# Linear-attention chunks with a MoE behind them: operands spread by matmuls in place of DRAM round trips, and more columns streamed ahead of the steps

## Chip, cores and metric

One core of a Trainium2 chip runs the whole program in one launch. The metric is device microseconds (us) of that core; the fewer the better.

## The reference

Three stages follow one another. The first is a recurrence over 768 time steps for 4 x 8 heads of width 40; the second a MoE layer with one of eight experts per token; the third a gated product with dense weights. Only the first stage is touched here.

```python
state = zeros(B, H, D, D)                     # 4, 8, 40, 40
for t in range(768):
    y[t]  = r[t] @ state
    Sa    = state @ a[t]
    state = state * w[t] - outer(Sa, b[t]) + outer(v[t], k[t])
x   = y reordered to (3072, 320)
x   = gate(x) * (relu(x @ w1[e(x)]) @ w2[e(x)])   # e(x): the expert of a token
out = ((x @ w_a) * (x @ w_b)) @ w_out
```

## The kernel before, in words

The recurrence is cut into 12 chunks of 64 time steps. Within a chunk the steps become matrix products: a Gram matrix of the decayed operands, the inverse of a triangular matrix made of it, and products with the state that the chunk before left. Each chunk `c` goes through these functions of the class `Attn`:

- `load` (L129) fetches the five operands `w a k b r` into tiles `raw0` to `raw4`, one buffer each. `cum` (L141) makes running products of `w` on VectorE (the scans of L151).
- `prod` (L164) multiplies `a`, `k`, `b` by these products (L174), splits each into two float16 halves (ScalarE: L177, L184, L191; GpSimd: L120, L185) and writes the halves from the tiles `ara`, `kb` and `arr` to DRAM (L171). Further DRAM writes are `dg` (L197) and `dds` (L205).
- `fetch` (L233) and `rfetch` (L214) read the halves back through `spread` (L211), three DMAs per tensor. The read puts them in another layout: a head's 40 rows stand three times, in the high-low pairing that the float16 products want, in the tiles `a3`, `kb3` and `r3`. `fetch` also reads `dds` into `DT` (L245), and `gtr` (L219) reads `dg` into `dl` (L222).
- `gram` (L248) makes the Gram matrix `gm` on TensorE (L256), masks it on VectorE (L257) and sends its diagonal blocks through DRAM (`tin`, L263, read back as `tl` by `tread`, L269) to be inverted on VectorE (`invert`, L271). The result goes through DRAM again (`td`, L290, read as `TT`, L294). `merge` (L296) joins the inverted blocks on TensorE, beginning with a transpose on VectorE (L298). `ztr` (L340) transposes `kb3`.
- `chain` (L361) in five steps C0 to C4 and `outs` (L421) in four steps O0 to O3 run once for each of four groups of heads `b`. C0 (X, L377, L380) needs the state `S3` that C3 of the chunk before left (L413), and C1 (L386) needs `TT`, so the chain is a recurrence over chunks.

The program is traced in an order written out by hand: `PLAN` (L504) gives each function a place in units of chunks, relative to its own chunk, and `run` (L478) sorts them. A scheduler then fixes the order on every engine and queue at build time, so an instruction whose input is late holds up all that stands behind it on its engine. All DMAs named here go through one queue, SP's. The PSUM tiles of `gram`, `ztr` and `gtr` come from one pool with two buffers (`pst`, L119).

`warm` (L356) streams columns of a constant tile through TensorE ahead of a step, into the PSUM tile that the step then overwrites. Its widths stand in `WARM`; index 5 is the Gram matrix, 1 to 4 and 6 are steps of `chain` and `outs`.

```python
KB,R3,A3,NZ,GT=1,3,3,4,2
WARM=(0,256,256,256,256,512,256)
```

After the chunks the MoE and the dense stage follow (class `Moe`); they are the same in both kernels.

Of the kernel before, what the change touches and what calls it, by code (L numbers as in the profile page):

```python
# [52 lines left out]
class Attn:  # L53
# [13 lines left out]
    def setup1(s):  # L67
        nc=s.nc; c=s.c
        if s.moe is None:
            s.idf=c.tile([128,128],F32,name="idf"); make_identity(nc,s.idf)  # L70
        else: s.idf=s.moe.idf
        s.idh=c.tile([128,128],F16,name="idh"); nc.vector.tensor_copy(s.idh,s.idf)
        s.tri=c.tile([128,64],F32,name="tri"); s.trg=c.tile([128,2,64],F32,name="trg")
        nc.gpsimd.memset(s.tri,1.0)
        for h in (0,1):
            v=s.tri[64*h:64*h+64]
            nc.gpsimd.affine_select(out=v,in_=v,compare_op=ALU.is_gt,fill=0.0,base=0,pattern=[[1,64]],channel_multiplier=-1)
        sc=-1.0/(AL*BE); ts=nc.vector.tensor_scalar
# [83 lines left out]
        s.load(c+1,0)  # L162
        yield
    def prod(s,c):  # L164
        nc=s.nc; V=nc.vector; d=s.ch[c]; raw=[d[('raw',n)] for n in range(5)]
        bf=d['bf']
        ar=[s.tile([128,2,6,128],F16,"ar"+n,f"ar{n}{c}",1) for n in "ar"]
        kb=s.tile([128,2,6,2,2,64],F16,"kb",f"kb{c}",KB)
        def out(t,n,w):
            dr=d['d'+n]=s.scr(n,[2,120,6,w],F16,c)  # L170
            nc.sync.dma_start(dr.rearrange("h r i t -> r h (i t)"),t[0:120])  # L171
        for (a,o) in ((2,2),(3,2),(1,0)):
            t=raw[a].rearrange("r (i h t) -> r h i t",h=2,t=32)
            (nc.gpsimd if c and a in s.PP else V).tensor_tensor(out=t,in0=t,in1=bf[:,o:o+2,:,o//2:o//2+32],op=ALU.mult)  # L174
            if a==1:
                src=raw[1].rearrange("r (i f) -> r i f",i=6)
                nc.scalar.activation(ar[0][:,0],src,AF.Copy)  # L177
                s.psub(ar[0][:,1],src,ar[0][:,0])
                out(ar[0].rearrange("r h i t -> r h (i t)"),"a",128)
            else:  # L180
                o0,ps=((64,64),(0,192))[a-2]
                src=sub(raw[a][:,0:1],0,[[128,6],[64,2],[1,64]])
                d0=sub(kb[:,0,0,0,0,0:1],o0,[[256,6],[ps,2],[1,64]]); d1=sub(kb[:,1,0,0,0,0:1],o0,[[256,6],[ps,2],[1,64]])
                nc.scalar.activation(d0,src,AF.Copy)  # L184
                nc.gpsimd.tensor_tensor(out=d1,in0=src,in1=d0,op=ALU.subtract)  # L185
                if a==3: out(kb.rearrange("r h i p s t -> r h (i p s t)"),"k",256)
            s.load(c+1,a)
            yield
        src=raw[4].rearrange("r (i f) -> r i f",i=6)
        V.tensor_scalar(out=raw[4],in0=raw[4],scalar1=RO,scalar2=None,op0=ALU.mult)  # L190
        nc.scalar.activation(ar[1][:,0],src,AF.Copy)  # L191
        s.psub(ar[1][:,1],src,ar[1][:,0])
        out(ar[1].rearrange("r h i t -> r h (i t)"),"r",128)
        s.load(c+1,4)

        dg=d['dg']=s.scr("g",[120,12,64],F32,c)
# [17 lines left out]
    def rfetch(s,c):  # L214
        d=s.ch[c]
        r3=d['r3']=s.tile([128,18,128],F16,"r3",f"r3{c}",R3)
        s.spread(r3,d['dr'],1)
        yield
    def gtr(s,c):  # L219
        nc=s.nc; d=s.ch[c]  # L220
# [3 lines left out]
        yield  # L224
        for hh in (0,1):
            pg=s.pst(f"pg{c}{hh}")
            n=4 if hh==0 else 2
            for i2 in range(n):
                tr=nc.tensor.transpose(pg[:,i2*120:i2*120+120], da[0:120,4*hh+i2].rearrange("p a t -> p (a t)"), s.idf[0:120,0:120])
                if i2==0: s.pin(tr)  # L230
            nc.scalar.activation(sub(gt[:,4*hh,0:1],0,[[240,3],[40,n],[1,40]]),sub(pg[:,0:1],0,[[40,3],[120,n],[1,40]]),AF.Copy)
            yield
    def fetch(s,c):  # L233
        nc=s.nc; d=s.ch[c]
# [3 lines left out]
        s.spread(a3,d['da'],2)  # L238
        yield
        s.spread(kb3.rearrange("e k p t -> e k (p t)"),d['dk'],1)  # L240
        yield
        if c>0:
            dds=d['dds']
            for p in (0,1):
                nc.sync.dma_start(s.DT[c%4][64*p:64*p+40].rearrange("e (j i) -> e j i",j=3),dds[p].rearrange("(j e) i -> e j i",e=40))  # L245
        yield
# [48 lines left out]
    def merge(s,c):  # L295
# [1 line left out]
        nc=s.nc; V=nc.vector; TT=s.TT[c%2]; T11=s.T11; gm=s.ch[c]['gm']; mm=nc.tensor.matmul; P1c=s.P1c  # L297
        s.pin(V.transpose(T11,TT[:,:,0:32]))  # L298
        yield
        pp=s.pmt(f"p0{c}",0)  # L300
        for k in range(16):
            for m in range(4):
                r=slice(32*m,32*m+32); o=32*(m%2)
                mm(pp[r,k*16:k*16+16],gm[r,k,m//2,o:o+32],T11[r,k,0:16],start=True,stop=True)
        nc.scalar.activation(P1c[:,:,0:16],pp.rearrange("p (q t) -> p q t",q=16),AF.Copy)
        yield
        pq=s.pmt(f"t1{c}",1)
        for k in range(16):
            for m in range(4):
                r=slice(32*m,32*m+32)  # L310
# [45 lines left out]
    def warm(s,ps,k):  # L356

        n=WARM[k]
        if n: s.nc.tensor.matmul(ps[:,0:n],s.sel[:,4],s.sel[:,0:4].rearrange("p a b -> p (a b)")[:,0:n],start=True,stop=True)

    def chain(s,c,b):  # L361
        nc=s.nc; V=nc.vector; d=s.ch[c]; mm=nc.tensor.matmul
# [112 lines left out]
        s.load_t(c); yield  # L475
    def run(s):

        for n in (0,2,3,1,4): s.load(0,n)  # L478
        ev=[]
        for c in range(s.NC):  # L480
            for nm,(n,a,b) in PLAN.items():
# [3 lines left out]
        def once(f):  # L485
            f(); yield
        ev.append((SETUP[0],-1,'s1',once(s.setup1)))
        if s.moe is not None:
            ev.append((-.8,-1,'s3',once(lambda: s.moe.early_loads(s.tile([128,320],F32,"y","ymoe",2)))))
            ev.append((s.NC-1.4,-1,'s4',once(lambda: s.moe.zero(s.tile([128,320],F32,"y","yzero",2)))))  # L490
# [571 lines left out]
```

## Time and profile before

| | us |
|---|---|
| median of 3 runs (1576.04 to 1589.54) | 1581.28 |
| the profiled execution | 1577.47 |
| its span, first to last instruction | 1575.7 |

TensorE is busy for 1198.2 us of the span, VectorE for 716.3, ScalarE for 530.3, GpSimd for 470.9. The profile cuts the span into slices and gives for each the busy share of each engine and the granted TensorE clock, where 1.00 stands for 2.4 GHz and 0.50 for 1.2 GHz. PE is TensorE's matmul side, PEld its weight loads, DVE VectorE, ACT ScalarE, POOL GpSimd, SP the engine whose queue issues the DMAs. In a row of instructions the bracket holds the idle time of the engine ahead of it and what ended it. The chunks take the first 875 us or so, the MoE and the dense stage the rest.

### The profile page before, as it was taken

What the parts mean: (1) busy time and instruction counts of PE and PEld (TensorE: products, weight loads), DVE (VectorE), ACT (ScalarE), POOL (GpSimd) and SP (SyncE); (2) the same over time, 40 slices, a digit from 0 to 9 for tenths busy, and PEclk for the clock granted to TensorE, in tenths of its full rate; (3) what the DMA queues carried; (4) which work ended last, traced back from release to release, by engine and by line L of the source; (5) the groups of instructions that cost most, each with busy time, mean ns of one, the idle gap of its engine ahead of it and who ended that gap; (6) DMA issues with size and microseconds to landing.
All of it is one profiled execution on the core that took longest, in us unless ns stands there. A gap on an engine that the chain in (4) does not pass through costs nothing. (4 is left out here: it accounts for less than half of the span.)

```text
span 1575.7 us, 34604 instructions
## 1 busy us (share of the span) xinstructions
PE 1198.2 (76%) x14569; PEld 1043.3 (66%) x14569; DVE 716.3 (45%) x1485; ACT 530.3 (34%) x1068; POOL 470.9 (30%) x434
## 2 busy tenths in 40 slices
PE   0111678955766877698987788887878999999998
PEld 0011567744655666587876687877867888989888
DVE  6552652533333333133324529999989321222211
ACT  5111434321524414343444124545423122131221
POOL 3533421321121301110114206656445232242221
PEclk9999976555756757757765798999989999999999
DMA  6888445454344343423232116777532000100000
GB/s 176 235 211 237 104 128 138 102 150 118 84 111 98 79 105 91 104 63 85 55 104 83 43 45 185 215 213 208 175 95 73 19 18 17 34 9 25 1 17 17
DMA packets 200117, 160.48 MB, mean 102 GB/s; under 512 B 128465, under 2 KB 168209, under 8 KB 199953
## 3 DMA queue, kind: packets, MB, share of 16 engines
q1 hardware_dynamic: 197553, 149.99, 35.8%
q0 software_dynamic: 2400, 8.20, 1.9%
q8 instruction: 116, 1.90, 0.5%
q14 instruction: 48, 0.39, 0.1%
HBM read 113.87 MB, written 44.27 MB: 100 GB/s over the span
## 5 line engine op out<-in xcount | busy, mean ns | idle before, releaser
L807 PE MATMUL ab<-X2H,abh 128*128 128x512 f32 x432 | 171.1, 398 | 4.3 <-DVE pr L997 3.9
L788 POOL TENSOR_TENSOR pL<-pr,pH 128x512 fp32r<-128x512 f32 x72 | 93.4, 1297 | 242.7 <-ACT pH L790 242.5
L807 PE MATMUL ab<-X2H,abl 128*128 128x512 f32 x432 | 121.6, 389 | 0.0
L997 DVE TENSOR_TENSOR pr<-ab,sa 128x512 f32<-128x512 f32 x72 | 49.6, 690 | 149.5 <-PE ab L807 149.5
L807 PE MATMUL ab<-X2L,abh 128*128 128x512 f32 x288 | 112.9, 394 | 0.0
L807 PE MATMUL ph<-XHb,w1h 128*128 128x256 f32 x312 | 89.7, 311 | 29.4 <-DVE hL L874 28.0
L256 PEld LDWEIGHTS <-kb 120*128 120x128 f16 x384 | 25.5, 124 | 130.6 <-issue 117.6
L256 PE MATMUL g<-a,kb 120*128 120x64 f16 x384 | 29.8, 232 | 102.9 <-DMA a<-da 70.7
L807 PEld LDWEIGHTS ab<-X2H,abh 128*128 128x128 f32 x432 | 82.1, 190 | 23.3 <-DVE pr L997 6.1
L790 ACT ACTIVATE pH<-pr 128x512 fp32r<-128x512 f32 x72 | 45.6, 633 | 144.0 <-DVE pr L997 132.4
L807 PEld LDWEIGHTS ab<-X2H,abl 128*128 128x128 f32 x432 | 81.1, 188 | 16.9
L1007 PE MATMUL po<-wol,pH 128*128 128x320 f32 x288 | 89.7, 312 | 1.5 <-POOL wol L788 1.5
L1007 PE MATMUL po<-woh,pH 128*128 128x320 f32 x288 | 89.5, 312 | 0.2 <-ACT woh L951 0.2
L788 POOL TENSOR_TENSOR w1l<-wr,w1h 128x512 fp32r<-128x512 f32 x51 | 71.1, 1408 | 59.9 <-ACT w1h L828 38.1
L1007 PE MATMUL po<-woh,pL 128*128 128x320 f32 x288 | 88.8, 311 | 0.0
L807 PEld LDWEIGHTS ph<-XHb,w1h 128*128 128x128 f32 x312 | 65.2, 210 | 35.6 <-DVE hL L874 29.5
L120 POOL TENSOR_TENSOR Q<-Qf,Q 128x320 f16<-128x320 f32 x48 | 38.0, 793 | 150.5 <-ACT Q L428 150.5
L996 ACT ACTIVATE sa<-ab 128x512 f32<-128x512 f32 x72 | 43.0, 597 | 113.5 <-PE ab L807 113.0
L174 POOL TENSOR_TENSOR raw<-raw,bf 128x768 f32<-128x768 f32 x22 | 38.8, 1764 | 131.8 <-DVE bf L151 48.0
L377 PE MATMUL x<-Qf,gm 64*64 64x40 f32 x768 | 57.2, 292 | 20.1 <-DVE Qf L354 20.1
L151 DVE TENSOR_TENSOR_SCAN bf<-raw,D 128x396 f32<-128x396 f32 x48 | 51.1, 1085 | 39.9 <-DMA dg<-bf 31.0
L884 PE MATMUL po<-w2h,hH 128*128 128x320 f32 x208 | 65.8, 319 | 2.9 <-ACT hH L873 2.9
(309 smaller groups left out, 3238.4 us busy)
## 6 DMA issues: line engine op xcount, KB each, us to landing
raw<-ct SPq DMA_DIRECT2D x48, 384.0 KB
kb<-dk SPq DMA_DIRECT2D x36, 360.0 KB
wr<-moe_w SPq DMA_DIRECT2D x40, 320.0 KB
wr<-moe_w SPq DMA_DIRECT2D x40, 256.0 KB
dk<-kb SPq DMA_DIRECT2D x12, 720.0 KB
a<-da SPq DMA_DIRECT2D x36, 180.0 KB
r<-dr SPq DMA_DIRECT2D x36, 180.0 KB
wr<-moe_w SPq DMA_DIRECT2D x40, 128.0 KB
```

The costliest lines, as they stand in the source:

```text
L120: def psub(s,out,a,b): s.nc.gpsimd.tensor_tensor(out=out,in0=a,in1=b,op=ALU.subtract)
L151: V.tensor_tensor_scan(o,i,d1.rearrange("p i t -> p (i t)"),0.0,ALU.mult,ALU.add)
L174: (nc.gpsimd if c and a in s.PP else V).tensor_tensor(out=t,in0=t,in1=bf[:,o:o+2,:,o//2:o//2+32],op=ALU.mult)
L256: nc.tensor.matmul(pg[:,(q*2+p)*64:(q*2+p)*64+64], d['kb3'][0:120,k,p], d['a3'][0:120,k,64*p:64*p+64], start=True,stop=True)
L377: mm(o(px,q,p),gm[r,k0+q,p],Q[r,p,q],start=not S,stop=not S or q==3)
L788: def psub(s,L,a,H): s.nc.gpsimd.tensor_tensor(out=L,in0=a,in1=H,op=ALU.subtract)
L790: s.nc.scalar.activation(H,src,AF.Copy)
L807: for i,(a,b) in enumerate(l): mm(o,a,b,start=(i==0),stop=(i==7))
L884: nc.tensor.matmul(po,a[:,m,tk],b[:,m],start=(k==0 and m==0 and n==0),stop=(k==3 and m==1 and n==2))
L996: sa=w.tile([128,512],F32,tag="sa",name=f"sa{g}{m}"); nc.scalar.activation(sa,pp[0],AF.Copy)
L997: pr=w.tile([128,512],F32,tag="pr",name=f"pr{g}{m}"); V.tensor_tensor(out=pr,in0=pp[1],in1=sa,op=ALU.mult)
L1007: nc.tensor.matmul(po,a[:,m,tk],b[:,m],start=(n==0),stop=(n==35)); n+=1
```

## The change

The halves are no longer written to DRAM. `spread` is rewritten: for each group of columns it runs two matmuls (high and low half) with a constant selection matrix `sps` as the stationary operand, and copies the result from PSUM to `kb3`, `a3` or `r3`, alternately on ScalarE and VectorE. `spr` does so for `kb3` and `a3`, `rspr` for `r3`, whose split is now a function of its own (`rprep`), placed later than before. `dds` is moved by six small matmuls and two ScalarE copies in `prod`, and `dg` by one GpSimd copy in `gtr`. `raw4` is loaded later in the first chunk. `WARM` is 512 throughout, and a new `warm2` streams 256-column matmuls ahead of the products of `merge`. `r3` has one buffer in place of three, `gt` four in place of two. `PLAN` places `cum` and `prod` later by 0.4 to 0.7 of a chunk.

```diff
-KB,R3,A3,NZ,GT=1,3,3,4,2
+KB,R3,A3,NZ,GT=1,1,3,4,4
-WARM=(0,256,256,256,256,512,256)
+WARM=(0,512,512,512,512,512,512)
 def setup1(s):
+        s.sps=c.tile([128,2,2,3,120],F16,name="sps"); nc.gpsimd.memset(s.sps,0.0)
+        for y,lo in ((0,2),(1,1)):
+            for g in range(3):
+                nc.vector.tensor_copy(s.sps[:,y,int(g==lo),:,40*g:40*g+40],s.idh[:,0:120].rearrange("p (j e) -> p j e",j=3))
 def prod(s,c):
-        def out(t,n,w):
-            dr=d['d'+n]=s.scr(n,[2,120,6,w],F16,c)
-            nc.sync.dma_start(dr.rearrange("h r i t -> r h (i t)"),t[0:120])
...
-        for h in (0,1): nc.sync.dma_start(dg[:,:,32*h:32*h+32],bf[0:120,h,:,0:32])
...
-            nc.sync.dma_start(dds.rearrange("p r i -> r p i"),dd[0:120].rearrange("r (p i) -> r p i",p=2))
+            pd=s.pst(f"pd{c}")
+            for j in range(3):
+                for p in (0,1): nc.tensor.matmul(pd[64*p:64*p+40,6*j:6*j+6],s.idf[0:120,40*j:40*j+40],dd[0:120,6*p:6*p+6],start=True,stop=True)
+            for p in (0,1): nc.scalar.activation(s.DT[c%4][64*p:64*p+40],pd[64*p:64*p+40,0:18],AF.Copy)
-    def spread(s,t,dr,lo):
-        for g in range(3):
-            s.nc.sync.dma_start(t[40*g:40*g+40].rearrange("e (j i) t -> e j (i t)",j=3),dr[int(g==lo)].rearrange("(j e) i t -> e j (i t)",j=3))
+    def spread(s,dst,src,y,w,nm):
+        nc=s.nc; n0=512//w; n=0
+        for j in range(3):
+            m=6 if j<2 else 4; st=n0 if m%n0==0 else 3
+            for i in range(0,m,st):
+                ps=s.pst(f"sp{nm}{j}{i}"); o=ps[0:120,0:st*w]
+                for h in (0,1): nc.tensor.matmul(o,s.sps[0:120,y,h,j],src[0:120,h,i:i+st].rearrange("r i t -> r (i t)"),start=h==0,stop=h==1)
+                d=dst[0:120,6*j+i:6*j+i+st]; o=o.rearrange("r (i t) -> r i t",i=st)
+                if n%2: nc.vector.tensor_copy(d,o)
+                else: nc.scalar.activation(d,o,AF.Copy)
+                n+=1
+                yield
+    def rspr(s,c):
+        r3=s.ch[c]['r3']=s.tile([128,18,128],F16,"r3",f"r3{c}",R3)
+        yield from s.spread(r3,s.ch[c]['rr'],1,128,f"r{c}")
 def gtr(s,c):
-        nc.sync.dma_start(da[0:120].rearrange("r i a t -> r (i a t)"),d['dg'].rearrange("r i t -> r (i t)"))
+        nc.gpsimd.tensor_copy(da.rearrange("r i p (h t) -> r h (i p) t",h=2),bf[:,0:2,:,0:32])
-    def fetch(s,c):
+    def spr(s,c):
...
+        yield from s.spread(kb3.rearrange("e k p t -> e k (p t)"),d['kb'].rearrange("r h i p s t -> r h i (p s t)"),1,256,f"k{c}")
+        yield from s.spread(a3,d['ar'],0,128,f"a{c}")
 def merge(s,c):
-        pp=s.pmt(f"p0{c}",0)
+        pp=s.pmt(f"p0{c}",0); s.warm2(pp,4)
-        pq=s.pmt(f"t1{c}",1)
+        pq=s.pmt(f"t1{c}",1); s.warm2(pq,4)
-            pp=s.pmt(f"p1{c}{b}",2*b)
+            pp=s.pmt(f"p1{c}{b}",2*b); s.warm2(pp,1)
-            pq=s.pmt(f"t2{c}{b}",2*b+1)
+            pq=s.pmt(f"t2{c}{b}",2*b+1); s.warm2(pq,1)
+    def warm2(s,ps,n):
+        for i in range(n): s.nc.tensor.matmul(ps,s.sel[:,4],s.sel[:,0:2].rearrange("p a b -> p (a b)"),start=True,stop=True)
-PLAN=dict(cum=(5,-3.456,-2.956),prod=(5,-2.906,-2.556),fetch=(3,-2.45,-2.3),...,gtr=(3,-0.9,-0.3),...,rfetch=(1,0.05,0.06),...)
+PLAN=dict(cum=(5,-2.75,-2.56),gtr=(3,-2.55,-2.35),prod=(4,-2.5,-2.26),spr=(13,-2.25,-1.97),...,rprep=(1,-0.3,-0.29),rspr=(5,0.06,0.3),...)
```

## Rows read from the trace of the kernel before

**Rows 1.** The page: granted clock in 40 slices, in tenths of full speed

```profile
PEclk9999976555756757757765798999989999999999
```

**Rows 2.** Busy us (x instructions) of each engine by stretch, then clock, DMA share, GB/s

```profile
0.00:160.00 160.00, 19.78 (x458) 14.69 (x459) 78.24 (x150) 43.80 (x62) 63.30 (x49) 1.00 0.80 213
160.00:875.00 715.00, 547.12 (x10464) 459.22 (x10461) 268.11 (x712) 269.02 (x599) 153.63 (x178) 0.66 0.40 100
```

**Rows 3.** Timeline of the first chunks by engine: POOL, PE, DVE, ACT (start us, us)

```profile
19.07 2.31 POOL L120 TENSOR_TENSOR ara<-raw,ara 128x768 f16<-128x768 f32 x1
...
50.61 1.01 PE L256 MATMUL g<-a,kb 120*128 120x64 f16 x16 [45.67 <-DMA a<-da]
...
52.81 0.61 PE L359 MATMUL g<-sel 128*128 128x512 f16 x1
53.22 0.63 PE L256 MATMUL g<-a,kb 120*128 120x64 f16 x8
...
142.99 1.91 PE L304 MATMUL p<-T,gm 32*32 32x16 f32 x128 [51.70 <-DVE T L298]
...
53.89 0.69 DVE L257 TENSOR_TENSOR gm<-g,trg 128x512 f32<-128x512 f32 x1 [0.16 <-PE g L256]
...
102.76 1.69 DVE L282 TENSOR_TENSOR tA<-tA,mA 128x14 f32<-128x14 f32 x1
...
163.90 0.30 ACT L380 ACTIVATE X<-x 128x160 f32<-128x160 f32 x1 [0.62 <-PE x L377]
```

**Rows 4.** SP's queue: two DRAM trips of chunk 0, then a later one

```profile
61.78 4.59 SPq L263 DMA_DIRECT2D tin<-gm  x8
80.18 0.34 SPq L269 DMA_DIRECT2D tl<-tin  x1
116.29 6.37 SPq L290 DMA_DIRECT2D td<-tA  x8
134.06 0.58 SPq L294 DMA_DIRECT2D TT<-td  x1
...
404.62 3.86 SPq L263 DMA_DIRECT2D tin<-gm  x8
411.36 0.34 SPq L269 DMA_DIRECT2D tl<-tin  x1
```

**Rows 5.** TensorE's largest wait from 160 to 875 us: total, times, longest

```profile
PE g L256 <- DMA kb<-dk: 27.8, 3, 11.7
```

**Rows 6.** Timeline of ScalarE and TensorE around two long waits

```profile
395.27 0.84 ACT L191 ACTIVATE arr<-raw 128x768 f16<-128x768 f32 x1 [18.74 <-DMA dr<-arr]
...
396.35 0.37 PE L359 MATMUL u<-sel 128*128 128x256 f16 x1 [14.45 <-ACT X L380]
...
480.45 0.84 ACT L191 ACTIVATE arr<-raw 128x768 f16<-128x768 f32 x1 [19.48 <-DMA dr<-arr]
...
481.98 0.37 PE L359 MATMUL S<-sel 128*128 128x256 f16 x1 [16.54 <-ACT Qf L389]
```

**Rows 7.** 512 columns at either clock: timeline, then the critical chain

```profile
425.00 0.63 PE L359 MATMUL g<-sel 128*128 128x512 f16 x1
425.43 0.63 PE L256 MATMUL g<-a,kb 120*128 120x64 f16 x8
...
1307.79 32.67 PE ab L807 x144
```

**Rows 8.** Two stretches with TensorE busy throughout, columns as in rows 2

```profile
622.50:646.40 23.90, 23.90 (x540) 20.42 (x539) 10.40 (x35) 13.63 (x33) 3.37 (x5) 1.00 0.26 58
680.50:711.20 30.70, 30.70 (x399) 26.10 (x395) 8.07 (x31) 13.31 (x32) 5.13 (x8) 0.50 0.39 92
```

**Rows 9.** Groups by line and shape: busy us, mean ns of one | idle before

```profile
L343 ACT ACTIVATE Z<-pz 128x480 f32<-128x480 f32 x24 | 13.6, 568 | 12.6 <-PE pz L341 12.4
...
L257 DVE TENSOR_TENSOR gm<-g,trg 128x512 f32<-128x512 f32 x48 | 32.6, 687 | 55.6 <-PE g L256 55.2
...
L174 POOL TENSOR_TENSOR raw<-raw,bf 128x768 f32<-128x768 f32 x22 | 38.8, 1764 | 131.8 <-DVE bf L151 48.0 <-DVE tA L282 32.3 <-DMA raw<-ct 26.3
```

More of the change, by code (lines that the diff above doesn't have):

```diff
@@ L164, in prod @@
     def prod(s,c):
-        nc=s.nc; V=nc.vector; d=s.ch[c]; raw=[d[('raw',n)] for n in range(5)]
+        nc=s.nc; V=nc.vector; d=s.ch[c]; raw=[d[('raw',n)] for n in range(4)]
         bf=d['bf']
-        ar=[s.tile([128,2,6,128],F16,"ar"+n,f"ar{n}{c}",1) for n in "ar"]
+        ar=s.tile([128,2,6,128],F16,"ara",f"ara{c}",1)
         kb=s.tile([128,2,6,2,2,64],F16,"kb",f"kb{c}",KB)
-        def out(t,n,w):
-            dr=d['d'+n]=s.scr(n,[2,120,6,w],F16,c)
-            nc.sync.dma_start(dr.rearrange("h r i t -> r h (i t)"),t[0:120])
+        d.update(kb=kb,ar=ar)
         for (a,o) in ((2,2),(3,2),(1,0)):
@@ L176, in prod @@
                 src=raw[1].rearrange("r (i f) -> r i f",i=6)
-                nc.scalar.activation(ar[0][:,0],src,AF.Copy)
-                s.psub(ar[0][:,1],src,ar[0][:,0])
-                out(ar[0].rearrange("r h i t -> r h (i t)"),"a",128)
+                nc.scalar.activation(ar[:,0],src,AF.Copy)
+                s.psub(ar[:,1],src,ar[:,0])
             else:
@@ L185, in prod @@
                 nc.gpsimd.tensor_tensor(out=d1,in0=src,in1=d0,op=ALU.subtract)
-                if a==3: out(kb.rearrange("r h i p s t -> r h (i p s t)"),"k",256)
             s.load(c+1,a)
             yield
[L189 to L196, printed above, removed]
-        for h in (0,1): nc.sync.dma_start(dg[:,:,32*h:32*h+32],bf[0:120,h,:,0:32])
         r32=s.tile([128,12],F32,"r32",f"r32{c}",2)
@@ L218, in rfetch, with rprep @@
+    def rprep(s,c):
+        nc=s.nc; raw=s.ch[c]['raw',4]
+        rr=s.ch[c]['rr']=s.tile([128,2,6,128],F16,"arr",f"arr{c}",1)
+        src=raw.rearrange("r (i f) -> r i f",i=6)
+        nc.vector.tensor_scalar(out=raw,in0=raw,scalar1=RO,scalar2=None,op0=ALU.mult)
+        nc.scalar.activation(rr[:,0],src,AF.Copy)
+        s.psub(rr[:,1],src,rr[:,0])
+        s.load(c+1,4)
         yield
+    def rspr(s,c):
+        r3=s.ch[c]['r3']=s.tile([128,18,128],F16,"r3",f"r3{c}",R3)
+        yield from s.spread(r3,s.ch[c]['rr'],1,128,f"r{c}")
@@ L219, in gtr @@
     def gtr(s,c):
-        nc=s.nc; d=s.ch[c]
+        nc=s.nc; d=s.ch[c]; bf=d['bf']
         da=s.tile([128,6,2,64],F32,"dl",f"dl{c}",1)
-        nc.sync.dma_start(da[0:120].rearrange("r i a t -> r (i a t)"),d['dg'].rearrange("r i t -> r (i t)"))
+        nc.gpsimd.tensor_copy(da.rearrange("r i p (h t) -> r h (i p) t",h=2),bf[:,0:2,:,0:32])
+        yield
         gt=d['gt']=s.tile([128,18,40],F32,"gt",f"gt{c}",GT)
-        yield
         for hh in (0,1):
@@ L237, in fetch @@
         d.update(a3=a3,kb3=kb3)
[L238 to L246, printed above, removed]
+        yield from s.spread(kb3.rearrange("e k p t -> e k (p t)"),d['kb'].rearrange("r h i p s t -> r h i (p s t)"),1,256,f"k{c}")
+        yield from s.spread(a3,d['ar'],0,128,f"a{c}")
     def gram(s,c):
@@ L476, in run @@
     def run(s):
-        for n in (0,2,3,1,4): s.load(0,n)
+        for n in (0,2,3,1): s.load(0,n)
         ev=[]
@@ L487, in run @@
         ev.append((SETUP[0],-1,'s1',once(s.setup1)))
+        ev.append((-1.7,-1,'s5',once(lambda: s.load(0,4))))
         if s.moe is not None:
@@ L499 @@
 SETUP=(-3.04,-2.3,.05)
-PLAN=dict(cum=(5,-3.456,-2.956),prod=(5,-2.906,-2.556),fetch=(3,-2.45,-2.3),gram=(5,-1.95,-1.8),tread=(1,-1.68,-1.67),ztr=(6,-1.85,-1.5),invert=(30,-1.5,-1.13),twrite=(1,-1.1,-1.09),tload=(1,-0.92,-0.91),gtr=(3,-0.9,-0.3),merge=(9,-0.7,-0.2),vpre=(4,-0.796,-0.088),rfetch=(1,0.05,0.06),C0=(4,-0.081,-0.071),C1=(4,-0.047,0.086),C2=(4,0.191,0.462),O0=(4,0.315,0.573),C3=(4,0.462,0.734),C4=(4,0.463,0.735),O1=(4,0.586,0.858),O2=(4,0.718,0.96),O3=(2,0.96,1.028))
+PLAN=dict(cum=(5,-2.75,-2.56),gtr=(3,-2.55,-2.35),prod=(4,-2.5,-2.26),spr=(13,-2.25,-1.97),gram=(5,-1.95,-1.8),tread=(1,-1.68,-1.67),ztr=(6,-1.85,-1.5),invert=(30,-1.5,-1.13),twrite=(1,-1.1,-1.09),tload=(1,-0.92,-0.91),merge=(9,-0.7,-0.2),vpre=(4,-0.796,-0.088),rprep=(1,-0.3,-0.29),rspr=(5,0.06,0.3),C0=(4,-0.081,-0.071),C1=(4,-0.047,0.086),C2=(4,0.191,0.462),O0=(4,0.315,0.573),C3=(4,0.462,0.734),C4=(4,0.463,0.735),O1=(4,0.586,0.858),O2=(4,0.718,0.96),O3=(2,0.96,1.028))
 NT=3072; NTI=24; D=320; E=8; F=1024; FF=1536; NB=13; NBT=21
```

12 lines of the change are left out of this document (2 added, 10 removed).

## The prediction

> **What bounds the kernel now.** I read the slices of the page first: the granted clock falls from the sixth slice on and stays near the middle until about the 22nd [rows 1]. The busy table by stretch, the second view, cuts the chunks into two parts there [rows 2]. Up to 160 us the DMA engines are 80% busy and TensorE works for 20 us. From 160 to 875 us DMA is at 40% and TensorE is busy for 547 of 715 us, at a mean clock of 0.66. VectorE and ScalarE are at 38% there, GpSimd at 21%. The 1.00 printed for the first stretch is not to be believed: a 512-column matmul at 52.81 has its successor at 53.22 [rows 3], 0.41 us, which is what the lower level gives further on [rows 7]. The column shows 1.00 where nothing was recorded.
>
> In the first part the bound is a path through DRAM. The last half that chunk 0 needs is ready on GpSimd at 21.4 us, but its Gram matmul starts at 50.6, released by the read of `a`; the first product of `merge` waits until 143.0 for the inverse [rows 3]. Between them SP's queue holds things up: `tin` is issued at 61.8, though its mask was done at 54.6 [rows 3], and its read-back only at 80.2, 13.8 us after the last write's issue; in a later chunk that distance is 2.9 us [rows 4]. Chunk 0's first X comes at 163.9 [rows 3], and from then on the chunks take some 59 us each, (875 - 164)/12.
>
> In the second part TensorE is the bound, at a low clock, with 168 us of idle time in it. The list of its waits names one cause outright, the read of `kb`: 27.8 us [rows 5]. Two more long waits look like ScalarE's fault, but the timeline shows ScalarE itself held in front of them by the split of `r`, which could not overwrite `arr` until that tile's DRAM write was through: 18.7 and 19.5 us, and TensorE's 14.5 and 16.5 us lie inside these [rows 6]. So 27.8 + 14.5 + 16.5 = 59 us of the 168 are DRAM trips. The stage behind the chunks I leave as it is.
>
> **The change part by part.** *DMA removed.* Per chunk 18 issues leave SP's queue (three writes of halves, nine reads, three for `dg`, three for `dds`) of some 46. With them go the holds above. For the first part: chunk 0 needs the spread of `kb3` and `a3`, 13 pairs of matmuls with 24 x 512 columns (counted below), for its Gram matrix. At 0.43 us each [rows 7] that is 10 us, of which some lie beside the last split. The Gram matrix then starts near 30 us in place of 50.6: 20 us gained. Without the SP holds the `tin` pair gives 11 us (13.8 against 2.9) and the issue of `tin` 7 (61.8 against 54.6). `td` is issued at 116.3 after an inversion that ends at 104.5 [rows 3, 4], 12 us, of which I take 10; `TT` is issued 11.4 us after the last `td`, against the same 2.9: 8 more. Sum 56 us. Low end 20 us (only the Gram matrix is earlier and VectorE, which has to scan and invert, is next); high end 75 us (the first X near 90 in place of 164). I take 55: each hold is seen, and VectorE at 78 of 160 us leaves room [rows 2]. For the second part I take the 59 us of idle time as gone; the ends are 0 (the next wait comes as late) and all 168, which I give no weight, since the steps of a chunk still wait for one another.
>
> *Columns added.* One chunk's spread is 16 matmuls of 512 columns for `kb3` and 8 x 384 + 2 x 512 for each of `a3` and `r3`: 16,384 columns. `WARM` adds 256 to each of 232 matmuls in the program (48 each for three steps, 88 for two), 59,392 columns. `warm2` adds 12 x 256 a chunk, 36,864. In all 196,608 + 59,392 + 36,864 = 292,864, or 572 times 512; two chunks' `kb3` and `a3`, 48 times 512, fall into the first part, where TensorE idles. The 524 left cost 225 us at 0.43 and 119 us at 32.67/144 = 0.227 us each [rows 7].
>
> *What they pay back.* The kernel's own mix runs at 540/23.9 = 22.6 matmuls per us at full clock and 399/30.7 = 13.0 at half [rows 8], a ratio of 1.74. A clock of 0.66 is full speed for 32% of the time, so 547 us are 547 x (1 + 0.74 x 0.32) = 677 us at half clock and 389 at full. With the added columns: 902 and 508. At a share h of full speed the busy time is 902/(1 + 0.776 h). The clock is the unknown. The change takes away stalls such as those of [rows 6] and adds long matmuls to every chunk, so I expect it to rise; how far, no row tells, and in the second stretch of [rows 8] TensorE worked throughout and had 0.50. I take a mean of 0.885, two thirds of the way to 1.00: h = 0.77, busy 565 us; I chose it as nearer to the first stretch of [rows 8], which is free of stalls, than to the present mean. Bounds: 0.80 (h = 0.6, 615 us) and 1.00 (508 us).
>
> *Evictions.* 18 copies a chunk, nine on ScalarE and nine on VectorE, at 0.57 to 0.69 us [rows 9]: 5 to 6 us per engine and chunk, beside TensorE, on engines 38% busy. If that cover is gone TensorE waits, since the PSUM pool has two buffers and TensorE goes in order: 0 to 0.69 us on each of 216 steps, 0 to 149 us. I take 0 beyond the idle time that stays, because two steps are in flight on two engines.
>
> *The rest.* The GpSimd copy for `gtr` is priced between 0.57 us (ScalarE's copy of 480 elements) and the 1.76 us of the multiply of that size [rows 9]; hidden, GpSimd being 21% busy [rows 2]; uncovered it would be 21 us at most. Six matmuls of six columns and two ScalarE copies of 18 for `dds` are far below the rows' sizes, and I leave them at nothing. `r3` in one buffer costs nothing where the matmuls that read it stand ahead of `rspr` in TensorE's own order; its copies then find it free. The constant `sps` is made once, while TensorE idles for lack of input, and the shorter lead of `PLAN` is paid out of the 55 us, not beside it. `rprep` moves one VectorE, one ScalarE, one GpSimd instruction and the load of `raw4` behind it; its split waits no more for a DRAM write but for matmuls of the chunk before.
>
> *Sum.* Second part: 565 + (168 - 59) = 674 against 715, a gain of 41 us. First part 55 us. The profiled execution's own 1577.5 - 41 - 55 = 1481.5, rounded to 1480 us. That execution lies 3.8 us below the median of 1581.3; I count from it. A measurement of this kernel tells about 1% from no change.
>
> **The rivals.** *A, the clock doesn't rise.* The columns are paid and the mean stays at 0.66: busy 902/(1 + 0.776 x 0.32) = 723 us, second part 832, so 117 us lost against 55 gained: 1640 us, slower. For it: a fully busy TensorE stays at half clock for 30 us [rows 8]. Against it: the sparse stretches are those without spread matmuls. It decides below a mean of 0.735 (h = 0.47: busy 661, and 661 + 109 = 770 is 715 + 55).
> *B, the base work doesn't speed up.* TensorE's small steps wait for ScalarE and VectorE whatever the clock: busy stays 547, the columns cost 119, the idle time is 109: 775 against 715, minus 55: 1582 us, no change. Against it: the ratio of 1.74 [rows 8]. The Trainium skill has a rule that would lead here: "TensorE: Matmul & The Clock Gate", section "What's actually happening", puts the ramp penalty under 1% of a typical kernel's span. By that rule the clock has almost nothing to give back and the sum is this rival's; the trace disagrees, with a mean of 0.66 over 715 us [rows 2], which is why the rival has a small chance.
> *C, evictions in the way.* Half of the bound of 149 us falls on TensorE's path: 1480 + 75 = 1555 us. For it: VectorE runs an inversion in long runs, and a copy behind it is late.
> *D, the waits come back in another form.* DRAM trips hidden by nothing else, yet loads or the `td` trip take their place, idle 168: 1480 + 59 = 1539 us.
>
> **How the numbers follow.** Forecast 0.56, A 0.11, B 0.04, C 0.10, D 0.19. The forecast's own ends: 615 + 109 with 20 gained gives 1566; 508 + 109 with 75 gained gives 1404. The range reaches from 1400 to 1575, which leaves out A, B and a little of C. Faster by over 1% means below 1562: the forecast but for 0.01, D but for 0.02, and 0.06 of C: 0.55 + 0.17 + 0.06 = 0.78. Within 1%: 0.01 + 0.02 + 0.03 + B = 0.10. Slower: A and 0.01 of C, 0.12.
>
> **What would show it.** Right: the first X on ScalarE before 120 us; no wait of TensorE for `kb` or `a` and none of ScalarE for a DMA write; a clock of 0.8 to 1.0 in the chunks' second part; the chunks over near 780 us; the stage behind as long as before. A clock near 0.66 there would make the price of the columns the story; waits of the spread matmuls for L343-like copies would mean C; a first X after 140 us would mean that VectorE, not DMA, set the start.

## The result, and the profile after

| | before | after |
|---|---|---|
| median, us | 1582.74 (4 runs beside it) | 1499.74 (4 runs, 1496.05 to 1506.08) |
| profiled execution, us | 1577.47 | 1497.71 |
| its span, us | 1575.7 | 1496.0 |
| mean granted clock of the span | 0.823 | 0.874 |

The ratio is 0.948, with a 95% interval from 0.9426 to 0.9534: some 5% faster, 20 us above the forecast of 1480 and inside its range. Some runs of four kernels further down were disturbed (one each of `columns_alone` and `g_copy_later`, most of `g_copy_later_narrow_columns` and `g_copy_and_merge_later`): their times are left out throughout, and the last two kernels have no interval.

The page of after, granted clock in 40 slices and DMA traffic (the first answers to [rows 1]):

```profile
PEclk9655997778869778897787999999799999999999
...
DMA packets 134697, 107.34 MB, mean 72 GB/s; under 512 B 86080, under 2 KB 111424, under 8 KB 134528
```

The middle that stood mostly at 5 to 7 stands mostly at 7 to 8 now and ends a slice earlier. The page of before has 200117 packets and 160.48 MB: a third of the traffic is gone.

The busy table of after by stretch (columns as in [rows 2]), cut where the first X is copied and where the last two ScalarE copies of the chunks begin; then the same of before with its own marks:

```profile
0.00:109.00 109.00, 58.37 (x638) 35.85 (x639) 80.43 (x173) 48.31 (x81) 45.61 (x40) 0.74 0.38 98
109.00:789.00 680.00, 612.04 (x10972) 444.48 (x10971) 286.94 (x787) 324.54 (x717) 179.43 (x195) 0.81 0.25 61
```

```profile
164.00:872.00 708.00, 540.81 (x10392) 453.52 (x10390) 264.15 (x701) 267.79 (x595) 152.33 (x177) 0.66 0.40 100
```

The start shrank from 164 to 109 us (-55), the chunks from 708 to 680 (-28), and the stage behind went from 704 to 707 (+3): together the 80 us between the spans. In the chunks TensorE is busy for 612 us instead of 541 and idle for 68 instead of 167. So 99 us of idle time went and 71 us of work came: the added work was paid only in part by the clock, which rose from 0.66 to 0.81.

The timeline of after in chunk 0, by engine (POOL, PE, DVE, ACT; it answers to [rows 3]):

```profile
21.52 0.82 POOL L231 COPY dl<-bf 128x768 f32<-128x768 f32 x1 [8.75 <-DVE bf L156]
22.30 2.30 POOL L125 TENSOR_TENSOR ara<-raw,ara 128x768 f16<-128x768 f32 x1
24.57 3.22 POOL L187 TENSOR_TENSOR kb<-raw,kb 128x768 f16<-128x768 f32 x2
27.84 1.01 PE L210 MATMUL spk<-kb,sps 120*120 120x512 f16 x2 [9.01 <-POOL kb L187]
...
33.42 2.69 DVE L156 TENSOR_TENSOR_SCAN bf<-raw,D 128x396 f32<-128x396 f32 x2
...
36.41 0.68 DVE L212 CAST kb<-spk 120x512 f16<-120x512 f32 x1
37.15 1.01 PE L210 MATMUL spk<-kb,sps 120*120 120x512 f16 x2 [2.57 <-DVE kb L212]
...
44.02 0.63 PE L257 MATMUL g<-a,kb 120*128 120x64 f16 x8
...
93.51 1.90 PE L305 MATMUL p<-T,gm 32*32 32x16 f32 x128 [0.59 <-DVE T L299]
...
109.21 0.30 ACT L383 ACTIVATE X<-x 128x160 f32<-128x160 f32 x1 [0.61 <-PE x L380]
```

and SP's queue in the same time (answers to [rows 4]):

```profile
47.47 5.02 SPq L264 DMA_DIRECT2D tin<-gm  x8
...
54.00 0.34 SPq L270 DMA_DIRECT2D tl<-tin  x1
...
81.26 3.81 SPq L291 DMA_DIRECT2D td<-tA  x8
...
86.59 0.57 SPq L295 DMA_DIRECT2D TT<-td  x1
```

Set against [rows 3, 4], step by step from mark to mark, this is where the 55 us come from (start of one row to the start of the next, before and after):

| step of chunk 0 | before | after | gain |
|---|---|---|---|
| to the first Gram matmul | 50.6 | 44.0 | 6.6 |
| Gram to the issue of `tin` | 11.2 | 3.5 | 7.7 |
| `tin` to `tl` | 18.4 | 6.5 | 11.9 |
| `tl` to `td` (the inversion, and SP's hold behind it) | 36.1 | 27.3 | 8.8 |
| `td` to `TT` | 17.8 | 5.3 | 12.5 |
| `TT` to the first product of `merge` | 8.9 | 6.9 | 2.0 |
| from there to the first X | 20.9 | 15.7 | 5.2 |

Three quarters of it, 40.9 us in the four middle steps, is SP's queue no longer holding things up. The Gram matrix itself gained little. GpSimd's copy of g for the next chunk (L231, at 21.5 us) had waited 8.75 us for VectorE, with chunk 0's own splits behind it, so the first spread started only at 27.8 us. But this hold isn't what set the Gram matrix: without it (`g_copy_later` below) the first spread starts 6 us earlier and the Gram matrix comes 1 us later. The spread itself took 16 us from its first matmul to the Gram matrix where the forecast had 10, largely because its PSUM tiles are copied out late. The longest such wait is in the timeline: two scans keep VectorE from 33.4 us on, the copy behind them comes at 36.4, and TensorE goes on at 37.2.

TensorE's largest waits in the chunks, after (answers to [rows 5]; us in total, times, longest), and then VectorE's largest:

```profile
PE p L305 <- DVE T L299: 11.7, 4, 3.9
PE p L305 <- DVE logits L586: 10.4, 1, 10.4
PE spa L210 <- DVE a L212: 10.4, 3, 4.9
PE n L360 <- DVE nf L443: 9.4, 3, 4.0
PE spa L210 <- DVE kb L212: 5.3, 1, 5.3
```

```profile
DVE T L299 <- DMA TT<-td: 66.2, 9, 14.4
```

There is no wait for `kb`, and none of ScalarE for a DMA write ([rows 6] have no answer). What is left names VectorE, and VectorE's own longest wait is for `TT`: 66.2 us in nine times. In the kernel before the same list holds this for the same line:

```profile
DVE T L298 <- DMA TT<-td: 11.8, 3, 5.3
```

One of the nine of after, in the timeline of after (SP's queue, VectorE, TensorE):

```profile
226.26 0.57 SPq L460 DMA_DIRECT2D xattn<-y  x1
...
228.83 3.58 SPq L461 DMA_DIRECT2D xe<-y  x1
232.59 3.02 SPq L295 DMA_DIRECT2D TT<-td  x1
...
243.24 0.71 DVE L299 STREAM_TRANSPOSE T<-TT 128x512 f32<-128x512 f32 x1 [14.43 <-DMA TT<-td]
243.87 0.13 DVE L586 TENSOR_TENSOR logits<-lg,bt 128x8 f32<-128x8 f32 x1
243.92 0.54 DVE L212 CAST a<-spa 120x384 f16<-120x384 f32 x1
...
244.00 0.29 PE L305 MATMUL p<-T,gm 32*32 32x16 f32 x4 [10.43 <-DVE logits L586]
```

VectorE reaches the transpose of `TT` at 228.8 us and stands there, because the read of `TT` is issued only at 232.6, behind four stores of `y`, and lands 10.7 us after its issue. TensorE stands for 10.4 us: its next instruction is the first product of `merge` (L305), which reads that transpose. The row names L586, which ended last before it. The eviction of a spread (L212) stands behind the transpose too. The granted clock on either side, from the busy table of after (the figure behind the five engines' busy times is the clock):

```profile
218.00:233.00 15.00, 15.00 (x266) 11.12 (x262) 6.83 (x22) 5.75 (x16) 4.42 (x4) 1.00 0.35 84
245.00:260.00 15.00, 15.00 (x199) 10.32 (x199) 5.65 (x10) 6.59 (x13) 9.85 (x10) 0.61 0.12 31
```

TensorE is busy throughout in both; ahead of the hold it runs at the upper level (2.4 GHz), behind it mostly at the lower one (1.2 GHz), 266 matmuls against 199. This hold was paid twice. But the clock falls without such a hold too. Later in the same trace TensorE is idle for 2.1 of 13.5 us, in gaps of at most 1.3 us, and then runs for 30.7 us at the lower level although it is busy throughout:

```profile
680.00:693.50 13.50, 11.39 (x376) 8.86 (x375) 2.98 (x7) 7.77 (x18) 3.86 (x5) 1.00 0.26 52
693.50:724.20 30.70, 30.65 (x405) 23.48 (x406) 11.38 (x42) 7.92 (x19) 1.40 (x3) 0.50 0.22 47
```

So the holds don't account for the whole of the low clock. And the wait for `TT` isn't what sets the time of the chunks: `merge_later` below is without it and no faster.

### The profile page after: what moved, and what is told of

Same layout as the page of the kernel before. It is cut to its first block, busy times and chain, and to the rows that moved or that the text cites. A ratio compares the mean times of both kernels' runs of the same rounds, so it can differ in the third digit from the quotient of the medians.

```text
span 1496.0 us, 35894 instructions
## 1 busy us (share of the span) xinstructions
PE 1299.5 (87%) x15277; PEld 1046.9 (70%) x15277; DVE 745.6 (50%) x1587; ACT 591.7 (40%) x1210; POOL 485.1 (32%) x447
## 5 line engine op out<-in xcount | busy, mean ns | idle before, releaser
L811 PE MATMUL ph<-XHb,w1h 128*128 128x256 f32 x312 | 88.7, 308 | 33.4 <-DVE hL L878 32.4
L210 PEld LDWEIGHTS <-sps 120*120 120x120 f16 x432 | 55.7, 157 | 74.2 <-issue 63.7
L210 PE MATMUL spk<-kb,sps 120*120 120x512 f16 x192 | 66.6, 460 | 26.5 <-DVE kb L212 9.9
L792 POOL TENSOR_TENSOR w1l<-wr,w1h 128x512 fp32r<-128x512 f32 x51 | 72.6, 1437 | 51.6 <-ACT w1h L832 49.4
L187 POOL TENSOR_TENSOR kb<-raw,kb 128x768 f16<-128x768 f32 x24 | 40.5, 1709 | 84.8 <-ACT kb L186 75.6
L811 PE MATMUL ph<-XLb,w1h 128*128 128x256 f32 x208 | 57.9, 305 | 10.9 <-DVE XLb L863 10.9
L334 POOL MEMSET TT<- 32x512 f32 x24 | 12.6, 523 | 168.7 <-PE p L331 168.1
L125 POOL TENSOR_TENSOR Q<-Qf,Q 128x320 f16<-128x320 f32 x48 | 42.6, 894 | 71.6 <-ACT Q L431 71.5
```

What stands on the lines that cost most here:

```text
L125: def psub(s,out,a,b): s.nc.gpsimd.tensor_tensor(out=out,in0=a,in1=b,op=ALU.subtract)
L210: for h in (0,1): nc.tensor.matmul(o,s.sps[0:120,y,h,j],src[0:120,h,i:i+st].rearrange("r i t -> r (i t)"),start=h==0,stop=h==1)
L792: def psub(s,L,a,H): s.nc.gpsimd.tensor_tensor(out=L,in0=a,in1=H,op=ALU.subtract)
L811: for i,(a,b) in enumerate(l): mm(o,a,b,start=(i==0),stop=(i==7))
```

## The experiments

All stretches are cut as above, from the copy of the first X to the last two copies of the chunks. The table has one line for each kernel; the profiled execution of each gives all but the first column.

| kernel | median us | first X | chunks | busy | idle | clock |
|---|---|---|---|---|---|---|
| before | 1583 | 164 | 708 | 541 | 167 | 0.66 |
| columns_alone | 1567 | 167 | 699 | 555 | 144 | 0.71 |
| second_buffer_for_r | 1585 | 166 | 712 | 536 | 176 | 0.65 |
| twelve_dram_slots | 1502 | 171 | 625 | 524 | 101 | 0.68 |
| twelve_slots_no_columns | 1508 | 170 | 632 | 495 | 137 | 0.61 |
| after | 1500 | 109 | 680 | 612 | 68 | 0.81 |
| spread_alone | 1491 | 108 | 674 | 605 | 69 | 0.73 |
| no_ahead_of_merges | 1502 | 108 | 686 | 608 | 78 | 0.77 |
| no_columns_at_all | 1460 | 102 | 648 | 566 | 82 | 0.70 |
| merge_later | 1495 | 97 | 687 | 612 | 75 | 0.80 |
| g_copy_later | 1449 | 113 | 636 | 596 | 40 | 0.83 |
| g_copy_later_no_columns | 1473 | 109 | 648 | 578 | 70 | 0.68 |
| g_copy_later_narrow_columns | 1465, one run | 111 | 646 | 584 | 62 | 0.76 |
| g_copy_and_merge_later | 1444 and 1461 | 106 | 651 | 605 | 46 | 0.82 |

### One part of the change at a time

`spread_alone` is the kernel after with the widths of before and an empty `warm2`:

```diff
-WARM=(0,512,512,512,512,512,512)
+WARM=(0,256,256,256,256,512,256)
-        for i in range(n): s.nc.tensor.matmul(...)
+        for i in range(0): s.nc.tensor.matmul(...)
```

> The changed kernel with the old widths (256 columns, 512 ahead of the Gram matrix) and nothing ahead of the merges: the spread by TensorE without the extra columns. My theory (start gained by the spread, the extra columns repaid by the clock): first X near 110 us as in the changed kernel, mean clock of the chunks' second part near 0.72 in place of 0.80, busy time there about as in the changed kernel, total 1500 to 1525 us. Rival (the extra columns are dead weight): clock still near 0.80, busy time some 40 us lower, total 1450 to 1475 us. Rival (all the gain comes from the columns): total 1550 us or more.

Measured: 1491.33 us, ratio 0.9417 (0.9367 to 0.9467). The busy table:

```profile
108.00:782.00 674.00, 604.73 (x10849) 463.75 (x10848) 286.75 (x789) 322.83 (x718) 178.39 (x195) 0.73 0.25 61
```

The total is below the expected range and at least as fast as the whole change; clock and busy time are as expected. The clock is 0.73 instead of 0.81, but 96,256 columns fewer run at it, and the busy time is 605 against 612 us. The added columns raise the clock and use up what it gives.

`columns_alone` is the converse, the kernel before with `WARM` at 512 and with `warm2` as in the change (4, 4, 1, 1):

> The kernel before, DRAM trips kept, with the widths 512 and the 256-column matmuls ahead of the merges. Added: 96,256 columns, 81 us at half clock, 43 at full. My theory: the stalls for DRAM trips stay, the first X stays near 164 us, the clock goes to some 0.72 to 0.76 and pays for the columns and no more: 1565 to 1595 us, no change. Rival (the columns alone lift the clock): 0.80 or more and 1540 us or less. Rival (dead weight): 0.66 and 1610 us or more.

Measured: 1566.73 us, ratio 0.9893 (0.9854 to 0.9932). The clock rose from 0.66 to 0.71, and 23 us of idle time went with 14 us of work coming. ScalarE's wait for the write of `arr` is still there, 51.6 us in four times. So the gain of the change isn't the columns'. It belongs to the rest of the change: the spread, its places in `PLAN` and its buffers, which these runs don't separate.

`no_ahead_of_merges` takes only `warm2` out of the kernel after (the second edit of `spread_alone`):

> The changed kernel without the 256-column matmuls ahead of the merges, widths of 512 kept. 36,864 columns less: 31 us at half clock, 16 at full. My theory: the clock falls by 0.01 to 0.03 and the total stays at 1490 to 1510 us. Rival (they are dead weight): 1480 us or less. Rival (they carry the rise of the clock): 1520 us or more.

Measured: 1502.37 us, ratio 0.9469 (0.9408 to 0.953), the same as after. The clock was 0.77, the busy time 608 us: the total doesn't tell whether these 36,864 columns are there.

`no_columns_at_all` also sets every width in `WARM` to 0, so no column is streamed for the clock anywhere in the chunks:

> The changed kernel with no streamed columns at all: width 0 everywhere and nothing ahead of the merges. Against the run with the old widths this takes 83,968 columns away (20 matmuls of 256 and 4 of 512 a chunk, less in the last): 71 us at half clock, 37 at full. If the columns pay for themselves and no more, as between the old widths and the new: clock near 0.66, busy time of TensorE in the chunks' second part 600 us within 15, total 1480 to 1505 us. Rival (the first columns carry the clock, the later ones don't): clock 0.60 or less and 1520 us or more. Rival (dead weight): 1470 us or less.

Measured: 1460.46 us, ratio 0.9244 (0.9202 to 0.9286), the expectation of dead weight. The busy table:

```profile
102.00:750.00 648.00, 566.25 (x10586) 449.33 (x10584) 283.87 (x794) 324.13 (x717) 178.18 (x196) 0.70 0.26 64
```

TensorE is busy 46 us less than in the kernel after although its clock is 0.70, and idle 14 us more. In this order of the work the columns that the kernel before already streamed cost 31 us, 6 of them ahead of the first X; those that the change added cost 8, which is not clear of the noise.

### What the DRAM trips really were

The prediction read ScalarE's long waits for the write of `arr` as a trip through DRAM that one more buffer, or no trip, would hide. `second_buffer_for_r` gives the kernel before that buffer, and takes one of the three of `r3` for it:

```diff
-KB,R3,A3,NZ,GT=1,3,3,4,2
+KB,R3,A3,NZ,GT=1,2,3,4,2
-        ar=[s.tile([128,2,6,128],F16,"ar"+n,f"ar{n}{c}",1) for n in "ar"]
+        ar=[s.tile([128,2,6,128],F16,"ar"+n,f"ar{n}{c}",1+int(n=="r")) for n in "ar"]
```

> The kernel before with a second buffer for the split halves of r (paid for with two buffers in place of three for the spread r). ScalarE need no longer wait for the DRAM write of the chunk before. My theory: the three waits of ScalarE for that write, 48.7 us in all, are gone, TensorE's two waits of 14.5 and 16.5 us behind them too, and the total falls by 20 to 35 us to 1545 to 1562 us. Rival (another wait takes the place): 1570 to 1590 us.

Measured: 1584.97 us, ratio 1.001 (0.9984 to 1.0035): nothing. ScalarE's waits in its chunks still hold this line:

```profile
ACT arr L191 <- DMA dr<-arr: 54.3, 4, 18.6
```

This run alone doesn't clear the tile, because it paid with a buffer of `r3`: the third chunk's read of `r` went out at 242 us instead of 92, and the seventh write behind it at 254 instead of 162. But it points at the slots in DRAM. In SP's queue of before the eighth write of `dr` follows the reads of the fourth chunk's `r`:

```profile
259.62 1.96 SPq L213 DMA_DIRECT2D r<-dr  x3
...
273.32 0.38 SPq L171 DMA_DIRECT2D dr<-arr  x1
```

The ninth to twelfth writes (321, 392, 476 and 554 us) follow the reads of the fifth to eighth chunks (which end by 315, 385, 468 and 548 us) in the same way: a write waits until one of four slots in DRAM has been read. `twelve_dram_slots` gives each chunk its own slot, for all four tensors, and changes nothing else:

```diff
-DB=dict(a=4,k=4,r=4,g=4)
+DB=dict(a=12,k=12,r=12,g=12)
```

> The kernel before with twelve DRAM slots per tensor in place of four, nothing else. After the run with a second buffer for r, whose splits still waited for the DRAM write, my theory is that the write itself waits for a slot: the fourth chunk back must have been read, and that read waits for a free r3. Then the three ScalarE waits of 48.7 us for the write, and TensorE's 14.5 and 16.5 us behind them, go with twelve slots: 1545 to 1565 us. Rival (the transfer is slow or something else is late then): ScalarE's waits for a DMA write stay over 30 us or TensorE's idle time stays, 1570 to 1590 us.

Measured: 1502.09 us, ratio 0.9489 (0.9436 to 0.9542), as much as the whole change, and more than was expected. The busy table, and TensorE's two waits for DMA in that stretch:

```profile
171.00:796.00 625.00, 524.06 (x10389) 442.47 (x10388) 237.44 (x687) 265.16 (x591) 143.34 (x172) 0.68 0.44 111
```

```profile
PE g L256 <- DMA DT<-dds: 15.6, 3, 12.8
PE g L256 <- DMA kb<-dk: 8.0, 1, 8.0
```

ScalarE's wait for `dr` is gone with a single `arr` tile, the wait for `kb` fell from 27.8 [rows 5] to 8.0 us, and the idle time from 167 to 101 us, with every transfer still made and the first X 7 us later than before. So most of the 59 us that the prediction put down to trips through DRAM were a ring of four slots. Which of the four tensors' slots matter, one run doesn't tell. With twelve slots the writes run up to seven chunks ahead of the reads, here the twelfth write and the fifth read of `r`:

```profile
294.25 0.39 SPq L171 DMA_DIRECT2D dr<-arr  x1
...
312.69 7.33 SPq L213 DMA_DIRECT2D r<-dr  x3
```

This also gives the change without its columns a fairer rival. Against twelve slots, `spread_alone` (the same widths) starts 63 us earlier (108 against 171) and needs 49 us more for the chunks (674 against 625): 81 us more of TensorE's time, 32 us less of idle time. Between these two kernels, which differ in `PLAN` and buffers too, the trip through DRAM is the cheaper way in the chunks, as long as the ring isn't full; at the start TensorE is.

`twelve_slots_no_columns` sets `WARM` to 0 in that kernel:

> Kernel before (operands through DRAM) with twelve slots of each operand in DRAM, which gave 1502, and with no columns streamed ahead of the steps. Theory, the columns are dead weight wherever TensorE bounds the chunks: on the spread by TensorE the same columns fewer (spread_alone against no_columns_at_all) were worth 31 us, so 1460 to 1485, which would put the trip through DRAM within some 20 us of the spread by TensorE. Rival, this kernel still waits for transfers and needs the columns for its clock: 1495 to 1520.

Measured: 1508.06 us, ratio 0.9554 (0.9515 to 0.9592): the rival. TensorE is busy 29 us less, at a clock of 0.61, and idle 36 us more. Here the same columns that cost 31 us beside the spread cost nothing that can be measured.

### The order of the work after the change

The change had also moved `gtr`, from -0.9 to -2.55 of a chunk. `g_copy_later` puts its copy, transposes and evictions 0.3 to 0.4 of a chunk later. It was meant for the start alone, so that GpSimd's copy of g no longer stands ahead of chunk 0's splits:

```diff
-gtr=(3,-2.55,-2.35)
+gtr=(3,-2.24,-1.96)
```

> The changed kernel with gtr placed behind prod in PLAN, so that on GpSimd the copy for chunk 1, which waits 8.75 us for VectorE's products, no longer stands ahead of the splits of chunk 0. My theory (that order costs the start its distance from the forecast 30 us): the first spread of the first chunk runs without the 9 us hold, the first Gram matmul comes near 34 us in place of 44, the first X 6 to 10 us earlier, the total 1488 to 1495 us. Rival (VectorE sets the start): first X within 3 us of the changed kernel's 109, total 1496 to 1504 us.

Measured: 1449.49 us (1437.66 to 1454.07), ratio 0.9144 (0.9081 to 0.9206). This is at least four times the gain expected, and not where it was expected. The first spread did start at 21.8 instead of 27.8 us, but its evictions on VectorE and the transposes of g then came in its way, the Gram matrix came at 45.1 instead of 44.0, and the first X at 113:

```profile
21.83 1.01 PE L210 MATMUL spk<-kb,sps 120*120 120x512 f16 x2 [3.44 <-POOL kb L187]
27.63 2.72 PE L210 MATMUL spk<-kb,sps 120*120 120x512 f16 x6 [4.79 <-DVE kb L212]
36.42 1.06 PE L238 MATMUL pg<-idf,dl 120*128 120x120 f32 x4 [6.08 <-DVE kb L212]
...
45.12 0.40 PE L257 MATMUL g<-a,kb 120*128 120x64 f16 x8
```

The gain is in the chunks. The busy table, TensorE's two largest waits there, and VectorE's wait for `TT`:

```profile
113.00:749.00 636.00, 596.10 (x10944) 434.32 (x10942) 288.69 (x787) 323.20 (x710) 177.39 (x194) 0.83 0.26 64
```

```profile
PE sr L420 <- DVE nf L443: 14.7, 7, 5.5
PE p L305 <- DVE T L299: 11.2, 4, 4.3
```

```profile
DVE T L299 <- DMA TT<-td: 30.4, 8, 6.4
```

VectorE waits for `TT` 30.4 us instead of 66.2, the waits of spread matmuls for evictions (15.7 us in the list of after) are gone, and TensorE has 40 us of idle time instead of 68. In this profile 5 gaps of TensorE are over 1.7 us, 19 us together; in that of after 16, 57 us together. There are fewer holds, a higher clock (0.83) and less busy time for the same columns. Which of the shifted instructions brought this about isn't shown; the next run says that it wasn't the shorter wait for `TT`.

`merge_later` gives `merge`, with VectorE's transpose of `TT` in it, a later place:

```diff
-merge=(9,-0.7,-0.2)
+merge=(9,-0.58,-0.15)
```

> The changed kernel with merge begun at -0.58 in place of -0.7 of a chunk. In the changed kernel VectorE stands in front of the transpose for the read of TT, 66 us in nine waits, and copies and masks stand behind it. My theory: that hold is the main stall left; most of the 66 us goes, TensorE's idle time in the chunks' second part falls from 68 to 45 us or less, the clock rises to 0.84 or more, the total is 1460 to 1485 us. Rival (the inverse is simply late, and the chain waits for it in another place): 1490 to 1510 us.

Measured: 1495.35 us, ratio 0.9482 (0.944 to 0.9525): no gain. The wait for `TT` did go, all 66.2 us of it: no such line is left among VectorE's waits in the chunks. TensorE's idle time didn't fall with it; it is 75 us instead of 68. The busy table, and TensorE's two largest waits now:

```profile
97.00:784.00 687.00, 611.74 (x11205) 445.40 (x11203) 293.65 (x793) 326.24 (x723) 184.63 (x198) 0.80 0.25 61
```

```profile
PE ut L434 <- POOL Q L125: 24.6, 5, 8.3
PE p L323 <- DVE T L315: 15.3, 8, 5.4
```

So the wait for `TT` was not the stall that sets the chunks' time: other waits took its place, as the rival had it. The first X came at 97 instead of 109 us and the chunks took 687 instead of 680, so more than half of the earlier start was given back.

Three kernels then asked whether these gains add up. `g_copy_later_no_columns` has the later copy of g and no streamed columns:

> Kernel after with two edits at once: the copies and transposes of g due later (as in g_copy_later, which gave 1452) and no streamed columns at all (as in no_columns_at_all, which gave 1460, against 1500 of the kernel after). Theory, two separate prices: what the streamed columns cost is TensorE's time, what the early copy of g costs is time in which TensorE waits for evictions that stand behind held work on VectorE and GpSimd, so the gains of 48 and 39 us add up: 1400 to 1425. Rival, one gain seen twice: with TensorE held less, its clock falls less, so the columns lose less; or without columns the engine has slack in which the copy's hold is hidden: 1440 to 1460.

Measured: 1472.51 us (1463.65 to 1482.76), ratio 0.9356 (0.9309 to 0.9403). That is neither range: with the copy later, leaving the columns out costs 23 us where it gained 39 before. TensorE is busy 18 us less (578), at a clock of 0.68, and idle 30 us more (70).

`g_copy_later_narrow_columns` has the widths of before and no columns ahead of the merges:

> Kernel after with the later copy of g and the widths of the kernel before (256 ahead of five of six, none ahead of the merges). Theory, two separate prices: spread_alone was 8 us under the kernel after, so 8 us under g_copy_later: 1436 to 1450, and above the run without any columns. Rival, with few waits the wide columns pay because they hold the clock: 1455 to 1475.

Measured: one run, 1465.44 us at a clock of 0.854. It lies with the rival and between the other two, but one run doesn't settle it.

`g_copy_and_merge_later` has both places changed and the columns of the kernel after:

> Kernel after with the later copy of g and the later merges together, columns as in the kernel after. Theory: the later merges alone brought the first X from 109 to 97 us and gave the 12 us back in the chunks, where evictions stood behind held work; with those waits gone by the later copy of g (1452) the earlier start is kept: 1434 to 1446, and the first X near 100 us. Rival: the chunks are set by TensorE's total work at the clock it gets, the start is given back whatever the order: 1448 to 1462.

Measured: runs of 1443.59 and 1460.73 us, one in the theory's range and one in the rival's; they can't be told from `g_copy_later`. In the profiled one, the slower, the first X came at 105.5 us, 7.5 earlier than there, and the chunks took 651 instead of 636: the earlier start was given back again, as the rival had it.

## Why the prediction was right, and where it was not

**The start: right in size, by other shares.** The forecast was 55 us and the first X near 109; it came at 109.2. That close a hit is luck. The Gram matrix gave 6.6 us where 20 were forecast: the working counted the spread's matmuls and left out what they wait for, above all evictions behind scans on VectorE. (GpSimd's copy of g ahead of chunk 0's splits also delayed the first spread, but taking it away brought the Gram matrix no earlier.) The SP holds gave more than their terms: 7.7 and 11.9 us around `tin` for 7 and 11, 12.5 for `TT` where 8 stood, 8.8 for `td` where 10 stood, and 7.2 us came from the last two steps, which had no term.

**The price of the work: right.** The formula 902/(1 + 0.776 h) gives 609 us at the measured clock of 0.81 (h = 0.62), and 612 were measured; for `g_copy_later`, which has the same columns, it gives 597 at 0.83, and 596 were measured. The base work does speed up with the clock, so rival B falls. By the same formula 612 us at 0.81 would be 508 at 1.00, so the lower level still costs some 7% of the span. The Trainium skill ("TensorE: Matmul & The Clock Gate", section "What's actually happening") puts the ramp penalty under 1% of a typical kernel's span; the trace of after disagrees for this kernel, by those 7%.

**The clock: the term that was mis-sized.** The step "I take a mean of 0.885" was wrong: 0.81, so 612 us of work in place of 565, 47 more. The choice leaned on a stretch free of stalls, and the kernel after still has 16 holds of over 1.7 us. That these alone keep the clock down isn't shown: it also stood at the lower level for 30.7 us from 693.5 us on, behind small gaps only. Rival A's end did not come: the clock rose well past its deciding point of 0.735.

**The idle time: mis-sized the other way.** Forecast 168 - 59 = 109 us, measured 68. The two errors nearly cancel in the chunks, 680 against 674 us, so the nearness of the total is luck there too. With the marks used here the chunks gained 28 us where 41 were forecast, and the stage behind took 3 us more: these 16 us are the difference between the 1481.5 of the sum and the 1497.7 of the profiled execution.

**The cause of the idle time: misread.** The step "27.8 + 14.5 + 16.5 = 59 us of the 168 are DRAM trips" named the right rows and the wrong cause. The runs show a ring of four DRAM slots: a second SBUF buffer, paid for with one of `r3`, gave nothing, and twelve slots took 66 us of idle time off with every trip still made.

**What the columns pay back: misjudged.** The forecast booked the added columns as part of what lifts the clock. They do lift it (0.73 to 0.77 to 0.81 from `spread_alone` through `no_ahead_of_merges` to after), and the busy time stays at 605 to 612 us all the while. Without them the kernel took 1491 us, without any columns 1460.

**C and D.** Evictions were costed at nothing beyond the idle time that stays; 15.7 us of spread matmuls waiting for VectorE's copies is what the list shows, far from the 75 of rival C. (The copies go ten to ScalarE and eight to VectorE in each chunk, not nine and nine: `spread` starts each tensor on ScalarE.) Of D one part came true: the `td` trip took the place of the others, with VectorE waiting 66.2 us for `TT`, but the sum of the idle time fell all the same, and taking that wait away gained nothing.

**The place of `gtr`: put at nothing.** The working priced GpSimd's copy of g at 0.57 to 1.76 us (0.82 was measured), called it hidden and bounded it by 21 us. Its price was right, but moving the copy with its transposes by 0.3 to 0.4 of a chunk was worth 50 us. What in that order cost so much stays open.

What stays open: why the columns cost 39 us with the early copy of g and are worth 23 with the late one. The shares of busy and idle time are shown, what ties the idle time to the columns is not. No run keeps the trips through DRAM under the change's `PLAN`, so what the later `cum` and `prod` gave is not separated from what the spread gave. A kernel with twelve slots that spreads by TensorE only in the first chunks was not tried. The fastest kernel measured with an interval is `g_copy_later`, 0.9144 of before and 50 us under the kernel after.

## What to carry to other kernels

When an engine waits for a DMA write, look at what that write itself waits for: a write that starts only after a read of several iterations back may be held by a full ring, and more slots are one number to try before the transfer is replaced by work on the engine that bounds the kernel. Columns streamed to hold TensorE's clock must be priced at the clock that is then measured, with a kernel that streams none as the control; a higher mean clock alone says nothing of the time. A long wait in a list is not yet a price: 66.2 us of VectorE's waits went here and the time stayed, so take the wait away before you believe it. And in a program in a fixed order, try other places: moving one small step (the copy and transposes of g) by a third of a chunk was worth more here than leaving out all columns.

## What was not expected of the hardware

A single hold of 10.4 us cost more than itself: in the 15 us cut out ahead of it TensorE had its full clock, in the 15 us cut out behind it a fully busy TensorE had 0.61. Yet a fully busy TensorE had 0.50 over 30.7 us with no long hold ahead of it either. And the mean clock of a run doesn't fix its time: `columns_alone` ran in 1566.15 us at 0.822 and in 1566.73 us at 0.868.
